# Attention and squared-ReLU feed-forward: fewer DMA transfers per pair of heads

## The chip, the cores and the metric

The kernel runs on one core of a Trainium2 chip. The metric is device time in microseconds (us) of one execution. A core has five engines that run side by side: TensorE (PE in the rows, its weight loads PEld), VectorE (DVE), ScalarE (ACT), GpSimd (POOL) and SyncE (SP), which here only issues DMA transfers. Data lie in DRAM, in the on-chip SBUF, and in the PSUM banks to which TensorE writes.

## The reference

```python
# q, k, v: 8 x 12 heads x 448 x 64; g_q, g_k: 64; w_in: 768 x 2048; w_out: 2048 x 768
def rmsnorm(x, g):
    return x / np.sqrt(np.mean(x * x, axis=-1, keepdims=True) + 1e-06) * g
q_n, k_n = rmsnorm(q, g_q), rmsnorm(k, g_k)
scores = np.matmul(q_n, k_n.transpose(0, 1, 3, 2)) / np.sqrt(64)
scores = scores - np.max(scores, axis=-1, keepdims=True)
attn = np.exp(scores)
attn = attn / (np.sum(attn, axis=-1, keepdims=True) + 1e-09)
attn_out = np.matmul(attn, v)
x = attn_out.transpose(0, 2, 1, 3).reshape(8 * 448, 768)
r = np.maximum(x @ w_in, 0.0)
out = (s * r * r + b) @ w_out
```

## The kernel before

The 96 heads are worked on in 48 pairs p, one head on SBUF partitions 0 to 63 and the other on 64 to 127. After attention come the two products of the feed-forward, `ffn_in` and `multiply`. The change touches attention alone.

Attention runs through slots i, four for each pair (`W = 4`). In a slot TensorE makes one of four blocks of scores (`score`, tile `sh`), VectorE takes the negative row maxima of it (`maximum`, tile `nmx`), TensorE makes a block of transposed scores in full precision and adds the maxima to it by a second matmul (`score_t`, tile `st`, from `kq` and `shq`), ScalarE takes the exponent (`exponent`, tile `e`), and in every odd slot TensorE multiplies two such blocks with `v` and with ones, which gives the sums (`weigh`, tile `av`). All instructions of an engine run in the order in which `slot` writes them. `score` runs up to `AHEAD = 10` slots ahead of `score_t`, because the maxima have to go from 112 partitions to one row of `shq` by two DMA transfers (`shift`, L253). `sh` has one buffer: the next scores wait until VectorE has read the last ones. `nmx` has two buffers, so the first maximum of pair p + 2 waits until both transfers of pair p have read their tile; `shq` has three.

What else a pair needs, in slots counted from its own, is set by `STAGES` and by the lines `at(...)`: the raw rows of k and q are loaded (`load`, L180, tile `raw`, two buffers), squared on ScalarE (L186) and summed on VectorE (L191); GpSimd makes 1/rms (`norm`, L193 and L194, tile `ri`), which goes to DRAM (`keep`, L197, `i_d`) and comes back spread over partitions (`spread`, L210, two transfers, tile `rb`, two buffers); k and q are also loaded transposed (`load_kq`, L204, tile `kq`, six buffers), multiplied by the norms on GpSimd (`scale`, L217) and rounded on ScalarE (L222, tile `kr`); v comes by L226. Afterwards ScalarE copies sums and products out of `av` (`take`, L303 and L304, tiles `sz` and `uz`), four small transfers bring the sums to 128 partitions (`gather`, L312, tile `zt`), VectorE inverts them (`invert`), they go to DRAM (`put_z`, L324) and come back spread (`get_z`, L329, two transfers, `zb`), GpSimd divides (`divide`, L335) and the result goes to DRAM (`put_x`, L338). Every second pair or so a piece of `w_in` is loaded (`convert`, L345) and split.

Every one of these transfers is issued by SyncE, one after the other, in the order of the code. A transfer has one of eight semaphores (DMAHW0 to DMAHW7), given out in turn; the queue that issues waits, where its semaphore is still taken, until the transfer that had it eight places before has landed. It also waits there for the engine that makes the data or frees the buffer, and everything behind it in the queue waits too.

Of the kernel before, what the change touches and what calls it, by code (L numbers as in the profile page):

```python
# [48 lines left out]
def attention_then_relu2_ffn(  # L49
    ctx: ExitStack,  # L50
    tc: tile.TileContext,
    kq: bass.AP,
    kq_rows: bass.AP,
    v: bass.AP,
# [11 lines left out]
    NPAIR, P, _, SEQ = kq.shape  # L66
    NT, DM = out.shape
    DF = w_in.shape[1]
    B = NT // SEQ
    D = P // 2  # L70
    NP = NPAIR // B
    TILES = 2 * SEQ // P
# [27 lines left out]
    x_d = [dpool.tile([NP, P, SEQ], F32, name=f"x_d{b}") for b in range(B)]  # L100
    z_d = [dpool.tile([2, SEQ], F32, name=f"z_d{p}") for p in range(NPAIR)]
# [53 lines left out]
    def attention(ps):  # L155
# [22 lines left out]
        def load(p):  # L178
            raw = raws[p] = ep.tile([P, 2, TILES, D], F32, tag="raw", bufs=2, name=f"raw{p}")
            nc.sync.dma_start(raw, kq_rows[p])  # L180
# [15 lines left out]
        def keep(p):  # L196
            nc.sync.dma_start(  # L197
                i_d[p].rearrange("t (p c) -> p t c", c=TILES),
                invs.pop(p).rearrange("p (t c) -> p t c", c=TILES),
            )  # L200

        def load_kq(p):
            t = kqs[p] = ap.tile([P, 2, SEQ], F32, tag="kq", bufs=6, name=f"kq{p}")
            nc.sync.dma_start(t, kq[p])  # L204

        def spread(p):
            rb = rbs[p] = ep.tile([P, 2, SEQ], F32, tag="rb", bufs=2, name=f"rb{p}")
            for j in range(2):
                r = i_d[p][:, j * SEQ : (j + 1) * SEQ].rearrange("(o t) s -> o t s", o=1)
                nc.sync.dma_start(rb[j * D : (j + 1) * D], r.broadcast_to([D, 2, SEQ]))  # L210

        def scale(p):
            t, rb = kqs[p], rbs.pop(p)
            S.activation(t[:, 1], t[:, 1], AF.Copy, scale=gqk)
            for n in range(2):
                E = V if p + n == 0 else G
                E.tensor_tensor(t[:, n], t[:, n], rb[:, n], ALU.mult)  # L217
# [5 lines left out]

        def load_v(p):
            t = vs[p] = ap.tile([P, NKC, 2, D], F32, tag="v", bufs=3, name=f"v{p}")
            nc.sync.dma_start(t, v[p])  # L226
# [13 lines left out]
        def maximum(i):  # L240
            p, c = divmod(i, W)
            if c == 0:
                nmxs[p] = ap.tile([QC, 2, NQ], F32R, tag="nmx", bufs=2, name=f"nmx{p}")
# [55 lines left out]
        def take(p):  # L299
            t = avs.pop(p)  # L300
            uz = uzs[p] = lp.tile([P, SEQ], F32, tag="uz", bufs=3, name=f"uz{p}")
# [4 lines left out]
        def gather(p):  # L306
            zt = zts[p] = lp.tile([P, 2, TILES], F32, tag="zt", bufs=2, name=f"zt{p}")
            sz = szs.pop(p)
            for j in range(2):
                for h in range(2):  # L310
                    n = (2 * h + j) * Q
                    nc.sync.dma_start(  # L312
# [508 lines left out]
```

## Time and profile before

| | |
|---|---|
| time, median of 3 runs | 1506.2 us (1504.15 to 1506.61) |
| time of the profiled execution | 1501.29 us |
| its span, first to last instruction | 1499.5 us |
| TensorE busy | 1399.3 us, 93% |
| VectorE, ScalarE, GpSimd busy | 759.2, 661.0, 622.0 us |
| mean granted TensorE clock | 0.973 |
| transfers by queue | all program transfers on one queue |

Busy time is the time in which an engine has an instruction under way; issuing transfers and waiting count for none. The attention part ends about 598 us after the first instruction; the feed-forward takes the rest. The time of an execution is 1.8 us longer than the span.

### The profile page before, as it was taken

To read this page: it belongs to the slowest core of one execution; us is meant where nothing else is said; L and a number is where in the kernel's file an instruction comes from. 1 tells how busy PE (TensorE), PEld (TensorE's weight loads), DVE (VectorE), ACT (ScalarE), POOL (GpSimd) and SP (SyncE) were. 2 spreads that over 40 slices of the span, in tenths; PEclk is the share of its full clock that TensorE was granted. 3 is DMA by queue.
4 is the path that set the end of the run, shared out by engine and by line. 5 is a ranking of instruction groups with operands and counts; after the bars stand their busy time and mean duration, and the time that the engine had idled before them with its cause. 6 is when DMAs were issued, how large, how long until landed. Compare 5 with 4: busy or idle time off the path is not lost. (4 is left out here: it accounts for less than half of the span.)

```text
span 1499.5 us, 23471 instructions
## 1 busy us (share of the span) xinstructions
PE 1399.3 (93%) x8536; PEld 1076.7 (72%) x8536; DVE 759.2 (51%) x1113; ACT 661.0 (44%) x1010; POOL 622.0 (41%) x536
## 2 busy tenths in 40 slices
PE   2799998888888999999999999999899999999999
PEld 2343443333333444799999999999799999999999
DVE  3465555555555653121222222224597777767775
ACT  3376566655656555222222222223554444444443
POOL 6466666666666652000000000004666546555653
PEclk6799999999999999999999999999999999999999
DMA  6567777767677774344434434434443324333331
GB/s 188 151 179 199 202 205 204 207 199 199 184 199 200 215 199 124 119 143 145 146 115 152 155 109 152 146 104 155 136 120 106 94 85 120 99 92 104 102 98 63
DMA packets 191235, 221.76 MB, mean 148 GB/s; under 512 B 69520, under 2 KB 162192, under 8 KB 191120
## 3 DMA queue, kind: packets, MB, share of 16 engines
q1 hardware_dynamic: 191120, 220.26, 49.7%
q8 instruction: 67, 1.10, 0.3%
q14 instruction: 48, 0.39, 0.1%
HBM read 161.48 MB, written 58.19 MB: 146 GB/s over the span
## 5 line engine op out<-in xcount | busy, mean ns | idle before, releaser
L439 PE MATMUL ph<-x,wih 128*128 128x448 f32 x1536 | 436.4, 365 | 1.1 <-ACT uz L304 1.1
L619 PE MATMUL m<-t,gh 128*128 128x384 f32 x1568 | 400.5, 336 | 7.3 <-ACT gh L600 7.3
L244 DVE TENSOR_REDUCE nmx<-sh 112x2 fp32r<-112x896 f32 x192 | 208.3, 1086 | 223.3 <-PE sh L235 107.6
L439 PEld LDWEIGHTS ph<-x,wih 128*128 128x128 f32 x1536 | 288.5, 188 | 24.7 <-ACT uz L304 1.9
L619 PEld LDWEIGHTS m<-t,gh 128*128 128x128 f32 x1568 | 284.5, 188 | 7.7 <-ACT gh L600 7.7
L439 PE MATMUL ph<-x,wil 128*128 128x448 f32 x768 | 280.5, 365 | 0.0
L275 ACT ACTIVATE e<-st 128x896 f32<-128x896 f32 x192 | 176.0, 917 | 216.0 <-PE st L268 215.6
L619 PE MATMUL m<-t,gl 128*128 128x384 f32 x784 | 263.3, 336 | 0.3 <-DVE gl L601 0.2
L457 ACT ACTIVATE r<-ph 128x448 f32<-128x448 f32 x128 | 69.6, 545 | 324.9 <-PE ph L439 175.3
L235 PEld LDWEIGHTS sh<-kr 64*112 64x112 f32 x384 | 54.2, 277 | 183.6 <-DVE nmx L244 77.3
L600 ACT CAST gh<-g 128x896 fp32r<-128x896 f32 x112 | 105.5, 943 | 177.9 <-POOL g L590 105.1
L527 POOL TENSOR_TENSOR w<-w 128x384 f32<-128x384 f32 x13 | 16.4, 1263 | 397.8 <-DMA w<-w_d 396.5
L264 PE MATMUL st<-kq 64*128 64x448 f32 x768 | 179.7, 544 | 0.0
L235 PE MATMUL sh<-kr 64*112 64x448 f32 x384 | 98.0, 507 | 83.2 <-DVE nmx L244 36.6
L285 PE MATMUL av<-e,v 128*32 128x448 f32 x1536 | 174.5, 574 | 0.0
L601 DVE TENSOR_TENSOR gl<-g,gh 128x896 fp32r<-128x896 f32 x112 | 141.9, 1268 | 57.2 <-ACT gh L600 52.4
L586 POOL TENSOR_TENSOR g<-g 128x256 f32<-128x256 f32 x112 | 94.5, 844 | 179.6 <-DVE g L585 179.6
L439 PEld LDWEIGHTS ph<-x,wil 128*128 128x128 f32 x768 | 144.2, 188 | 11.4
L619 PEld LDWEIGHTS m<-t,gl 128*128 128x128 f32 x784 | 147.5, 188 | 1.2 <-DVE gl L601 1.2
L268 PE MATMUL st<-shq,row 64*128 64x448 f32 x384 | 139.2, 717 | 3.1 <-DMA shq<-nmx 3.1
L430 DVE TENSOR_TENSOR x<-xr,x 128x448 fp32r<-128x448 f32 x48 | 30.4, 635 | 207.9 <-ACT x L429 207.9
L590 POOL TENSOR_TENSOR g<-g 128x256 f32<-128x256 f32 x112 | 133.9, 1196 | 0.0
(64 smaller groups left out, 1452.1 us busy)
## 6 DMA issues: line engine op xcount, KB each, us to landing
r_d<-r SPq DMA_DIRECT2D x128, 224.0 KB, 2.0
raw<-in_dram SPq DMA_DIRECT2D x48, 448.0 KB, 6.1
kq<-in_dram SPq DMA_DIRECT2D x48, 448.0 KB, 3.8
rb<-i_d SPq DMA_DIRECT2D x96, 224.0 KB, 5.1
raw<-r_d SPq DMA_DIRECT2D x64, 256.0 KB, 2.8
v<-in_dram SPq DMA_DIRECT2D x48, 256.0 KB, 2.9
w64i<-in_dram SPq DMA_DIRECT2D x24, 512.0 KB, 5.1
w64o<-in_dram SPq DMA_DIRECT2D x32, 384.0 KB, 3.3
```

The source lines that it names most:

```text
L235: T.matmul(sh[:QC, j, :SEQ], t[d, 1].rearrange("k (p c) -> k c p", c=NQ)[:, c], t[d, 0], start=True, stop=True,)
L244: V.tensor_reduce(out=nmxs[p][:, :, c : c + 1], in_=shs.pop(i)[:QC, :, :SEQ], op=ALU.max, axis=AX.X, negate=True,)
L264: T.matmul(st[:, j, :SEQ], t[d, 0, k0 : k0 + P], t[d, 1], start=True, stop=False)
L268: T.matmul(st[:, j, :SEQ], row[d], shq[p % 3][d], start=False, stop=True)
L275: S.activation(e, sts.pop(i)[:, :, :SEQ], AF.Exp)
L285: T.matmul(t[n * Q : (n + 1) * Q, 0, :SEQ], x[:, 2 * g + h, j, m * Q : (m + 1) * Q], e[h][:, j], start=g + h == 0, stop=g + h == 2,)
L439: T.matmul(ph[:, :SEQ], w[:, cc, f0 : f0 + P], xs[b, cc][:, part, :], start=cc == 0 and n == 0, stop=cc == NCC - 1 and n == 2,)
L586: G.tensor_tensor(g9[:, 2:4], g9[:, 0:2], g9[:, 7:8].broadcast_to([P, 2, P]), ALU.add)
L590: G.tensor_tensor(g9[:, 5:7], g9[:, 0:9:8], g9[:, 1:8:6], ALU.subtract)
L600: S.copy(gh, g9[:, 1:8])
L601: V.tensor_tensor(gl, g9[:, 1:8], gh.bitcast(F32), ALU.subtract)
L619: T.matmul(to, g[:, sa], w, start=m == 0 and n == 0, stop=m == NM - 1 and n == 2,)
```

## The change

Six edits, all in attention. (1) The four transfers of `gather` become two: the four rows of `sz` go to a new DRAM tile `s_d`, and two slots later a new function `fetch` reads them to 128 partitions; `invert` to `put_x` come two slots later, and `uz` gets a fourth buffer. (2) The transposed k and q and the v of a pair lie side by side in DRAM and come in one load of 5632 bytes for each partition; `load_v` is gone, and v stays in the `kq` tile, which is now used until the last `weigh` of its pair. (3) From pair 4 on the raw rows are loaded by ScalarE's queue instead of SyncE's. (4) The norms go to DRAM in one run of 14 numbers for each partition instead of two of 7, in another order; `spread` reads one run for each partition, and `scale` reads `rb` with a stride. (5) `nmx` gets four buffers instead of two. (6) Slots go on for two more steps of the feed-forward.

```diff
--- before.py
+++ after.py
@@ -98,6 +96,7 @@
 
     r_d = [dpool.tile([NFC, P, SEQ], F32, name=f"r_d{b}") for b in range(B)]
     x_d = [dpool.tile([NP, P, SEQ], F32, name=f"x_d{b}") for b in range(B)]
+    s_d = [dpool.tile([4, SEQ], F32, name=f"s_d{p}") for p in range(NPAIR)]
     z_d = [dpool.tile([2, SEQ], F32, name=f"z_d{p}") for p in range(NPAIR)]
     w_d = [dpool.tile([2, P, 2, DM // 2], F32, name=f"w_d{m}") for m in range(NFC // 2)]
     i_d = [dpool.tile([2, 2 * SEQ], F32, name=f"i_d{p}") for p in range(NPAIR)]
@@ -177,7 +176,7 @@
 
         def load(p):
             raw = raws[p] = ep.tile([P, 2, TILES, D], F32, tag="raw", bufs=2, name=f"raw{p}")
-            nc.sync.dma_start(raw, kq_rows[p])
+            (nc.sync if p < 4 else nc.scalar).dma_start(raw, kq_rows[p])
 
         def norm(p):
 
@@ -195,35 +194,35 @@
 
         def keep(p):
             nc.sync.dma_start(
-                i_d[p].rearrange("t (p c) -> p t c", c=TILES),
-                invs.pop(p).rearrange("p (t c) -> p t c", c=TILES),
+                i_d[p].rearrange("j (p n) -> (j p) n", n=2 * TILES), invs.pop(p)
             )
 
         def load_kq(p):
-            t = kqs[p] = ap.tile([P, 2, SEQ], F32, tag="kq", bufs=6, name=f"kq{p}")
-            nc.sync.dma_start(t, kq[p])
+            t = ap.tile([P, 2 * SEQ + 2 * NKC * D], F32, tag="kq", bufs=6, name=f"kqv{p}")
+            nc.sync.dma_start(t, kqv[p])
+            kqs[p] = t[:, : 2 * SEQ].rearrange("p (n s) -> p n s", n=2)
+            vs[p] = t[:, 2 * SEQ :].rearrange("p (c j d) -> p c j d", j=2, d=D)
 
         def spread(p):
-            rb = rbs[p] = ep.tile([P, 2, SEQ], F32, tag="rb", bufs=2, name=f"rb{p}")
+            rb = rbs[p] = ep.tile([P, 2 * SEQ], F32, tag="rb", bufs=2, name=f"rb{p}")
             for j in range(2):
-                r = i_d[p][:, j * SEQ : (j + 1) * SEQ].rearrange("(o t) s -> o t s", o=1)
-                nc.sync.dma_start(rb[j * D : (j + 1) * D], r.broadcast_to([D, 2, SEQ]))
+                nc.sync.dma_start(
+                    rb[j * D : (j + 1) * D], i_d[p][j : j + 1].broadcast_to([D, 2 * SEQ])
+                )
 
         def scale(p):
-            t, rb = kqs[p], rbs.pop(p)
+            t = kqs[p]
+            rb = rbs.pop(p).rearrange("p (s t c) -> p t s c", t=2, c=TILES)
             S.activation(t[:, 1], t[:, 1], AF.Copy, scale=gqk)
             for n in range(2):
                 E = V if p + n == 0 else G
-                E.tensor_tensor(t[:, n], t[:, n], rb[:, n], ALU.mult)
+                of = t[:, n].rearrange("p (s c) -> p s c", c=TILES)
+                E.tensor_tensor(of, of, rb[:, n], ALU.mult)
             yield
             yield
             yield
             kr = krs[p] = ep.tile([P, 2, SEQ], F32R, tag="kr", bufs=2, name=f"kr{p}")
             S.copy(kr, t)
-
-        def load_v(p):
-            t = vs[p] = ap.tile([P, NKC, 2, D], F32, tag="v", bufs=3, name=f"v{p}")
-            nc.sync.dma_start(t, v[p])
 
         def score(i):
             p, c = divmod(i, W)
@@ -240,7 +239,7 @@
         def maximum(i):
             p, c = divmod(i, W)
             if c == 0:
-                nmxs[p] = ap.tile([QC, 2, NQ], F32R, tag="nmx", bufs=2, name=f"nmx{p}")
+                nmxs[p] = ap.tile([QC, 2, NQ], F32R, tag="nmx", bufs=4, name=f"nmx{p}")
             V.tensor_reduce(
                 out=nmxs[p][:, :, c : c + 1], in_=shs.pop(i)[:QC, :, :SEQ],
                 op=ALU.max, axis=AX.X, negate=True,
@@ -298,21 +297,17 @@
 
         def take(p):
             t = avs.pop(p)
-            uz = uzs[p] = lp.tile([P, SEQ], F32, tag="uz", bufs=3, name=f"uz{p}")
+            uz = uzs[p] = lp.tile([P, SEQ], F32, tag="uz", bufs=4, name=f"uz{p}")
             sz = szs[p] = lp.tile([P, SEQ], F32, tag="sz", bufs=2, name=f"sz{p}")
             S.copy(sz, t[:, 1, :SEQ])
             S.copy(uz, t[:, 0, :SEQ])
 
         def gather(p):
+            nc.sync.dma_start(s_d[p], szs.pop(p)[0:P:Q])
+
+        def fetch(p):
             zt = zts[p] = lp.tile([P, 2, TILES], F32, tag="zt", bufs=2, name=f"zt{p}")
-            sz = szs.pop(p)
-            for j in range(2):
-                for h in range(2):
-                    n = (2 * h + j) * Q
-                    nc.sync.dma_start(
-                        zt[j * D : (j + 1) * D, h],
-                        sz[n : n + 1].rearrange("o (p c) -> o p c", c=TILES),
-                    )
+            nc.sync.dma_start(zt, s_d[p].rearrange("(h j) (p c) -> (j p) h c", h=2, c=TILES))
 
         def invert(p):
             zt = zts[p]
@@ -366,13 +361,13 @@
             ):
                 at(max(slot_of(s0) + off, FIRST + least + p), f, p)
             at(slot_of(s0 + W - 1) + (p > 0), shift, p)
-            at(max(s0 - 4, FIRST + 10), load_v, p)
             at(s0 + 7, gather, p)
-            at(s0 + 10, invert, p)
-            at(s0 + 11, put_z, p)
-            at(s0 + 13, get_z, p)
-            at(s0 + 16, divide, p)
-            at(s0 + 18, put_x, p)
+            at(s0 + 9, fetch, p)
+            at(s0 + 12, invert, p)
+            at(s0 + 13, put_z, p)
+            at(s0 + 15, get_z, p)
+            at(s0 + 18, divide, p)
+            at(s0 + 20, put_x, p)
         for n in range(len(pieces)):
             at(8 + 7 * n, convert, n)
 
@@ -700,7 +695,7 @@
             rectify()
             ffn_in(b, fc)
             keep_r()
-            if n < 20:
+            if n < 22:
                 slot(NSLOT + 2 + n)
             else:
                 begun[:] = [g for g in begun if next(g, 0) is None]
@@ -803,7 +798,8 @@
 
     vs[:, : p // 2, 3] = 0
     g = _np.stack([_np.tile(_np.asarray(inputs[x]), 2) for x in ("g_q", "g_k")], 1)
-    laid = [kq, rows, vs, g] + [_np.asarray(inputs[x]) for x in _INS]
+    kqv = _np.concatenate([a.reshape(n, p, -1) for a in (kq, vs)], 2)
+    laid = [kqv, rows, g] + [_np.asarray(inputs[x]) for x in _INS]
     arrays, args = {}, []
     for i, a in enumerate(laid):
         a = _np.ascontiguousarray(a)
```

SyncE's queue, before, from the spread norms of pair 14 to the sums of pair 8 (names end in a buffer number of the build; `x2` is a repetition; in brackets the semaphores that the queue waits for ahead of the transfer: DMAHW is an earlier transfer, the others are engines):

```order
L210 DMA rb_1439<-i_d_161 64x2x448 [waits DMAHW6_49,Pool_49]
L210 DMA rb_1439<-i_d_161 64x2x448 [waits DMAHW7_49]
L180 DMA raw_1442<-in_dram 128x896 [waits DMAHW0_49,DVE_49]
L338 DMA x_d_83<-u_1413 128x448 [waits DMAHW1_49,Pool_49]
L253 DMA shq_217<-nmx_1345 1x112x4 [waits DMAHW2_49,DVE_49]
L253 DMA shq_217<-nmx_1345 1x112x4 [waits DMAHW3_49,PE_49]
L197 DMA i_d_162<-ri_1377 128x2x7 [waits DMAHW4_49]
L324 DMA z_d_98<-zt_1381 128x7 [waits DMAHW5_49,DVE_49]
L312 DMA zt_1498<-sz_1457 64x1x7 [waits DMAHW6_49,Activation_49]
L312 DMA zt_1498<-sz_1457 64x1x7 [waits DMAHW7_49]
L312 DMA zt_1498<-sz_1457 64x1x7 [waits DMAHW0_49]
L312 DMA zt_1498<-sz_1457 64x1x7 [waits DMAHW1_49]
```

The same place now, from the load of pair 14 on:

```order
L202 DMA kqv_1422<-in_dram 128x1408 [waits DMAHW6_49,PE_49]
L340 DMA w64i_1424<-in_dram 128x1024 [waits DMAHW7_49]
L319 DMA z_d_145<-zt_1325 128x7 [waits DMAHW0_49,DVE_49]
L310 DMA zt_1439<-s_d_98 128x2x7 [waits DMAHW3_49,DMAHW1_49]
L209 DMA rb_1444<-i_d_209 64x896 [waits DMAHW2_49]
L209 DMA rb_1444<-i_d_209 64x896
L252 DMA shq_265<-nmx_1354 1x112x4 [waits DMAHW4_49,DVE_49]
L252 DMA shq_265<-nmx_1354 1x112x4 [waits DMAHW5_49]
L196 DMA i_d_210<-ri_1385 128x14 [waits DMAHW6_49,Pool_49]
L324 DMA zb_1501<-z_d_145 64x448 [waits DMAHW7_49,DMAHW0_49]
L324 DMA zb_1501<-z_d_145 64x448
L306 DMA s_d_99<-sz_1462 4x448 [waits DMAHW1_49,Activation_49]
```

The loads of `v` and `raw` and two of the four `zt` transfers are gone from the queue, `s_d` is new, and the one load `kqv` waits for TensorE: for the last matmul with v of the pair six before, which stands one slot later in the program than the load.

ScalarE's instructions, before, from the scaling of the `kq` of pair 14, in the odd slot in which the sums and products of pair 9 are copied out of `av`:

```order
L214 ACTIVATE kq_1417<-kq_1417,gqk 128x448 [waits DMAHW2_49]
L303 COPY sz_1571<-av_1503 128x448 [waits DMAHW6_49,DMAHW5_49,DMAHW7_49,DMAHW0_49,PE_49]
L304 COPY uz_1570<-av_1503 128x448 [waits Pool_49]
L275 ACTIVATE e_1584<-st_1579 128x896 [waits PE_49,Activation_49]
L110 ACTIVATE wih_223<-w64i_1419 128x512 [waits DMAHW3_49]
L186 ACTIVATE raw_1442<-raw_1442 128x896 [waits DMAHW0_49]
L275 ACTIVATE e_1601<-st_1596 128x896 [waits PE_49,Activation_49]
```

And now:

```order
L216 ACTIVATE kqv_1422<-kqv_1422,gqk 128x448 [waits DMAHW6_49]
L179 DMA raw_1557<-in_dram 128x896 [waits DMAHW3_49,DVE_49]
L302 COPY sz_1572<-av_1505 128x448 [waits PE_49]
L303 COPY uz_1571<-av_1505 128x448 [waits Pool_49]
L274 ACTIVATE e_1585<-st_1580 128x896 [waits PE_49]
L109 ACTIVATE wih_271<-w64i_1424 128x512 [waits DMAHW7_49]
L185 ACTIVATE raw_1447<-raw_1447 128x896 [waits DMAHW5_49]
```

The load of `raw` (pair 18) stands between the scaling of `kqv` and the two copies out of `av`; it waits for VectorE, which has to have summed the buffer's last rows, and for DMAHW3, which the transfer eight places before has, counted over both queues: here the second `rb` of pair 14. Of the 44 such loads 22 stand behind an `rb`, 11 behind an `shq`, 6 behind a `w64i`.

## Rows read from the trace of the kernel before

**Rows 1.** Windows: busy us (instructions) by engine, clock, DMA share, GB/s; stages.

```profile
0.00:85.00 85.00, 45.09 (x284) 25.67 (x284) 36.34 (x43) 32.19 (x41) 42.63 (x43) 0.76 0.59 166
85.00:125.00 40.00, 40.00 (x322) 18.35 (x320) 27.58 (x36) 28.71 (x40) 29.65 (x20) 1.00 0.72 199
125.00:545.00 420.00, 372.19 (x2772) 163.07 (x2770) 237.52 (x323) 250.39 (x353) 264.64 (x195) 0.96 0.72 200
500.00:550.00 50.00, 45.81 (x350) 20.31 (x342) 28.97 (x39) 29.02 (x42) 30.06 (x23) 0.97 0.79 212
545.00:598.00 53.00, 52.65 (x424) 22.84 (x420) 23.64 (x36) 30.63 (x42) 15.78 (x13) 1.00 0.52 154
598.00:1499.50 901.50, 889.38 (x4750) 846.73 (x4748) 434.16 (x678) 319.10 (x535) 269.29 (x268) 1.00 0.38 119
```

**Rows 2.** Waits from 125 to 545: us in total, times, longest.

```profile
DVE nmx L244 <- DMA shq<-nmx: 98.2, 24, 6.1
...
PEld sh L235 <- DVE nmx L244: 65.2, 32, 4.1
```

**Rows 3.** Timeline of TensorE's `av` matmuls, ahead of a wait and behind it.

```profile
307.81 1.71 PE L285 MATMUL av<-e,v 128*32 128x448 f32 x16
...
316.21 2.95 PE L285 MATMUL av<-e,v 128*32 128x448 f32 x16
```

**Rows 4.** Timeline of SyncE's queue, one pair: start, us, transfers.

```profile
449.80 0.53 SPq L226 DMA_DIRECT2D v<-in_dram  x1
450.42 0.38 SPq L204 DMA_DIRECT2D kq<-in_dram  x1
450.89 1.10 SPq L329 DMA_DIRECT2D zb<-z_d  x2
452.08 1.27 SPq L210 DMA_DIRECT2D rb<-i_d  x2
453.44 1.44 SPq L180 DMA_DIRECT2D raw<-in_dram  x1
454.97 0.38 SPq L338 DMA_DIRECT2D x_d<-u  x1
455.45 1.24 SPq L253 DMA_DIRECT2D shq<-nmx  x2
456.74 0.58 SPq L197 DMA_DIRECT2D i_d<-ri  x1
457.38 0.46 SPq L345 DMA_DIRECT2D w64i<-in_dram  x1
457.93 0.38 SPq L324 DMA_DIRECT2D z_d<-zt  x1
458.40 3.13 SPq L312 DMA_DIRECT2D zt<-sz  x4
461.63 0.53 SPq L226 DMA_DIRECT2D v<-in_dram  x1
```

**Rows 5.** Transfers from 125 to 545: count, KB each, median us from issue to landing.

```profile
rb<-i_d SPq DMA_DIRECT2D x69, 224.0 KB, 5.2
...
zt<-sz SPq DMA_DIRECT2D x140, 1.8 KB, 2.9
shq<-nmx SPq DMA_DIRECT2D x70, 1.8 KB, 5.8
```

**Rows 6.** Groups of instructions on GpSimd, 600 to 1499: busy us, mean ns.

```profile
L590 POOL TENSOR_TENSOR g<-g 128x256 f32<-128x256 f32 x112 | 133.9, 1196 | 0.0
```

**Rows 7.** The same view from 125 to 545.

```profile
L217 POOL TENSOR_TENSOR kq<-kq,rb 128x448 f32<-128x448 f32 x70 | 83.3, 1209 | 9.9 <-PE st L268 3.3 <-ACT kq L214 2.8 <-DMA rb<-i_d 2.4
```

**Rows 8.** Timeline of the start: first scores, first shift, first use of it.

```profile
22.25 0.94 ACT L222 CAST kr<-kq 128x896 fp32r<-128x896 f32 x1 [0.16 <-POOL kq L217]
...
38.17 1.23 SPq L253 DMA_DIRECT2D shq<-nmx  x2
...
44.10 1.01 PE L268 MATMUL st<-shq,row 64*128 64x448 f32 x2 [3.11 <-DMA shq<-nmx]
```

More of the change, by code (lines that the diff above doesn't have):

```diff
@@ L51, in attention_then_relu2_ffn @@
     tc: tile.TileContext,
-    kq: bass.AP,
+    kqv: bass.AP,
     kq_rows: bass.AP,
-    v: bass.AP,
     g_qk: bass.AP,
@@ L64, in attention_then_relu2_ffn @@
     V, S, G, T = nc.vector, nc.scalar, nc.gpsimd, nc.tensor
-    NPAIR, P, _, SEQ = kq.shape
     NT, DM = out.shape
     DF = w_in.shape[1]
+    NPAIR, P, _, TILES, D = kq_rows.shape
+    SEQ = TILES * P // 2
     B = NT // SEQ
-    D = P // 2
     NP = NPAIR // B
-    TILES = 2 * SEQ // P
     NQ = 4
```

## The prediction

> **What bounds the kernel now.** I read the windows by stage first [rows 1]. The feed-forward, from 598 us on, has TensorE busy 889.4 of 901.5 us at full clock, and the change does not touch it. The start, 0 to 85, is a chain of loads and norms. Between lie two kinds of attention. From 85 to 125 TensorE is busy all of 40.0 us and gets through 322 matmuls; a pair has 80 (8 `sh`, 16 and 8 `st`, 32 and 16 `av`), so a pair takes 10.0 us. From 545 to 598, 424 matmuls in 53 us: again 10.0 us for a pair. Between them, from 125 to 545, 2772 matmuls take 420 us. That is 34.65 pairs of 12.12 us. All three stretches hold the same work for TensorE, and the first has the pieces of `w_in` in it too, so 10.0 us is what TensorE needs and 34.65 x 2.12 = 73.5 us are lost in the middle.
>
> The same row says how: 420 - 372.2 = 47.8 us TensorE is idle, and the other 25.7 us are work that took longer. The granted clock is 0.96 there and 1.00 in the stretches beside it, and behind an idle time the 16 `av` matmuls take 2.95 us in place of 1.71 [rows 3]: the lower of the two levels, 1.2 in place of 2.4 GHz, for a while after each longer wait. So a wait costs about half as much again as it lasts, and both parts go if it goes.
>
> What TensorE waits for is VectorE's maximum (65.2 us of waits ahead of `sh`), and VectorE in turn waits 24 times, 98.2 us, up to 6.1 us each, for the transfers of `shift` [rows 2]: the first maximum of a pair finds both `nmx` buffers taken, because the shift of the pair two before has not read its tile. That shift was due four slots earlier. It is late because SyncE's queue is full [rows 4]: from one `v` load to the next are 11.83 us, and transfers stand end to end in them, 10.89 us with gaps of some 0.1 us between. Two places in it are waits rather than issue: `raw` has 1.44 us where `v`, a load of the same kind, has 0.53, and the four `zt` 3.13 us. A shift also needs 5.8 us from issue to landing though it carries 1.8 KB [rows 5]; it stands behind the large loads.
>
> **The change part by part.** Off SyncE's queue, per pair, by the durations of [rows 4]: the `v` load, 0.53; the `raw` load, 1.44 with its wait (0.53, as `v`, without); two of four `zt`, 1.57 (3.13 / 2). `s_d` and the new `zt` count as the two that stay. With four gaps of 0.1 that is 3.0 to 3.9 us less of 11.83, so 7.9 to 8.8 us for a period that needs 10.0. The merged `kqv` load is priced between 0.38 and 0.53 (the `kq` and `v` rows); the store of norms at most its 0.58, the rows of half the count. I take 8.5 us: SyncE falls below TensorE, and the slack is 1.5 us a pair.
>
> `nmx` with four buffers removes the wait itself: the first maximum of a pair now needs the shift of the pair four before, eight slots (some 20 us) more. What is late next is TensorE's second `st` matmul, which needs the shifted row in `shq`, six slots or 15 us after the shift's place. With 5.8 us to land that allows SyncE to run 9 us late. So with the queue at 8.5 us of 10.0 I put both stalls at nothing.
>
> New waits. The `kqv` load has to wait until TensorE has done the last `av` of the pair six before, one slot after its own place, so SyncE runs at least a slot (2.5 us) behind once a pair. Behind it stand `z_d`, `zt`, both `rb`, both `shq`, `i_d`. They have the 9 us above (`shq`), and `rb` is issued about 3 us after the release and lands at 8.2 (5.2 in [rows 5]), ahead of the multiplication four slots after it, at 10. Cost nothing, up to 0.6 us a pair if the larger load in front delays them. The sums now go by two transfers in sequence. The first is bounded by the small ones of [rows 5], 2.9 and 5.8 us, and the second follows two slots (5 us) behind: at most 0.8 us of wait, inside SyncE's slack; the second has three slots (7.5 us). Nothing.
>
> ScalarE issues `raw` itself: 0.38 to 0.53 us, as `kq` and `v` on SyncE [rows 4], on an engine that is busy 250.4 / 34.65 = 7.2 us a pair [rows 1]; hidden in the 2.8 us that are left of 10.0. But it also waits there, ahead of the two copies out of `av`, for a transfer of SyncE's. ScalarE comes there some 10 us after the `kqv` release of the pair before; the second `rb`, 22 loads of 44, has landed at 8.2, so no wait; an `shq`, 11 loads, is issued near 4.3 and lands at 10.1: a wait of a few tenths to 1 us. Averaged with the delays above I put 0.15 us a pair on it, bounds 0 and 0.6.
>
> GpSimd multiplies with a strided `rb`. Nothing here shows that form. Contiguous it takes 1209 ns for 448 elements [rows 7]; the dearest strided one, in the feed-forward, 1196 ns for 256 [rows 6], which would be 2.09 us for 448. GpSimd is busy 264.6 / 34.65 = 7.6 us a pair; twice 0.88 more is 9.4, still below 10.0. I take the lower, since the runs of seven stay contiguous; the upper one goes into the range.
>
> The start: the first `kr` ends at 23.2, the first shift is issued at 38.2 and lands at 44.1, when TensorE can go on [rows 8]. The early `kqv` loads carry 256 KB more each, at the 166 GB/s of that stretch 1.5 us, and ScalarE's two extra waits stand ahead of its first `kr`. Against it SyncE has two `raw` loads less ahead of the first shift. I take +2 us, bounds -5 and +6.
>
> Sum, against the profiled execution: 34.65 pairs x (12.12 - 10.15) = 68.3 us less, 2 more at the start: 1501.3 - 68.3 + 2 = 1435.0 us. The median of the three runs, 1506.2, lies 4.9 above the profiled one; stalls of varying length would do that, and most are to go, so I add 2: **1437 us**.
>
> **A rule against it.** The DMA share is 0.72 from 125 to 545 [rows 1], which leaves room, while SyncE's queue has none [rows 4]; the sum above goes by that. The Trainium skill, "DMA: Bandwidth & Descriptors", section "Issuing engines are not separate DMA queues", says that transfers of all issuing engines share the same 16 DMA engines, and that another issuer saves only the sequencer's time, "usually small relative to the DMA itself". Here that time is the larger part, as rows 4 show; were it small, the move of `raw` would bring nothing and the merged load its half microsecond alone. No run here yet shows which holds once the queue is relieved; it is the first rival.
>
> **The rivals.** (a) The transfers themselves become the bound. The DMA engines are busy 0.72 x 420 / 34.65 = 8.7 us a pair; at 10.0 that would be 0.87, and the fullest 50 us show 0.79 [rows 1]. If 0.79 is as far as it goes, a pair takes 8.7 / 0.79 = 11.05 us: 34.65 x 1.07 = 37 us less, and with the start 1466. Against it: the merged loads and the norms' longer runs need fewer packets for the same bytes. This is the rule's case. Chance 0.25, 1448 to 1482.
>
> (b) The change does not do what it says: SyncE's waits grow by what the issues shrink, because the eight semaphores allow only eight transfers under way, and the period stays at 11.8 or so; TensorE then waits for `shq` in place of `sh`. For it: the waits in `zt` and `raw`. Against: 13.6 transfers a pair take the place of 16.6. 34.65 x 0.1 to 0.5: 1485 to 1503. Chance 0.06.
>
> (c) Slower: ScalarE stands at the `raw` load. Its period is 7.2 + 0.5 + the wait. It is as long as now when the wait is 4.4 us, that is when an `rb` needs 10 - 3 + 4.4 = 11.4 us to land where 5.2 are seen. At 12.5 us the pair takes 13.2, 34.65 x 1.1 = 38 us more: 1540. For it: `kqv` and `raw` are issued at nearly the same time, 1152 KB together, and all small transfers stand behind. Against: a landing time twice what any row shows. Chance 0.07.
>
> **How the numbers follow.** The forecast, a pair of 10.0 to 10.4 us, has 0.60; with its bounds (73.5 less and 5 at the start; 0.4 x 34.65 = 14 and 6 more) it runs from 1423 to 1448. The remaining 0.02 is for less than that. To leave out no more than two in ten the range takes in (a): 1424 to 1480. Faster by over 0.2% (3 us, about what a measurement of this kernel can tell from no change): 0.60 + 0.25 + 0.05 of (b), and 0.01 of the rest, 0.91. Within 0.2%: 0.02. Slower: 0.07.
>
> **What would show it.** Right: the 2772 matmuls of the middle in about 350 us, clock near 1.00, no wait of VectorE for `shq<-nmx`, gaps in SyncE's queue ahead of each `kqv`, ScalarE's wait at the `raw` load below 1 us. (a) shows a DMA share near 0.8 with landing times well above those of rows 5; (b) SyncE without gaps and TensorE waiting at `st` for `shq`; (c) ScalarE idle at that load and TensorE idle at `av` or `st` behind it. Two things would make the forecast wrong without any of these: a start much longer than 85 us, and GpSimd's strided product near 2 us with the waits around it.

## The result, and the profile after

The changed kernel takes 1446.5 us (median of 4 runs, 1442.0 to 1450.5) where the kernel before takes 1505.2 on the same chip (1499.7 to 1506.6): a ratio of 0.9616, with an interval of 0.9572 to 0.9659. The forecast was 1437, in a range of 1424 to 1480. The profiled execution took 1443.12 us; the forecast's sum for it was 1435.0. In one kernel of the table below, e10_raw_later, two of six executions fell into a slower state of the chip (1555.6 and 3523.5 us) and are left out of its numbers.

The windows by stage come first, as for before in [rows 1]; the middle is cut at 500 here, because the last 45 us of it run free of stalls now.

```profile
core 0: us, PE busy (x) PEld busy (x) DVE busy (x) ACT busy (x) POOL busy (x), PEclk, DMA share, GB/s
0.00:85.00 85.00, 44.83 (x278) 25.43 (x280) 35.75 (x40) 31.97 (x41) 41.37 (x43) 0.76 0.61 177
85.00:125.00 40.00, 40.00 (x322) 18.48 (x322) 26.99 (x36) 28.56 (x40) 29.80 (x22) 1.00 0.75 219
125.00:500.00 375.00, 359.56 (x2864) 168.35 (x2868) 247.32 (x333) 258.36 (x363) 298.45 (x197) 1.00 0.80 229
500.00:545.00 45.00, 45.00 (x370) 19.13 (x362) 18.06 (x28) 25.10 (x35) 11.65 (x10) 1.00 0.39 112
```

Between 125 and 500 there are 2864 matmuls, 35.8 pairs of 10.47 us, where a pair took 12.12. The 34.65 pairs that the forecast counted take 57.2 us less by that, and the profiled execution is 58.2 us shorter: nearly the whole gain lies in the middle. The start is much what it was (278 matmuls in the first 85 us, 284 before). The granted clock of the middle is 1.00 again (0.96 before), and TensorE's busy time is 359.56 / 35.8 = 10.04 us a pair, the 10.0 that the forecast said it needs. What is left of the loss is idle time alone: 375 - 359.56 = 15.4 us.

The waits from 125 to 545 say who holds it (us in total, times, longest; to be read against [rows 2]):

```profile
DVE nmx L243 <- PE sh L234: 87.6, 119, 1.8
...
DVE zt L314 <- DMA zt<-s_d: 37.2, 22, 3.9
POOL u L330 <- DMA zb<-z_d: 34.6, 17, 8.7
...
POOL kqv L220 <- DMA rb<-i_d: 26.2, 18, 3.9
...
PE sh L234 <- DVE nmx L243: 12.9, 13, 2.0
...
DVE zt L314 <- DMA rb<-i_d: 9.1, 7, 2.9
```

VectorE's 98.2 us of waits for `shq` are gone; its maxima wait for TensorE's scores, as they should. It waits instead at `invert` (line 314) for the sums that now come by way of DRAM, 22 times, up to 3.9 us. The 9.1 us that the view puts down to `rb` are waits for the sums too: the instruction reads `zt` alone. I went through TensorE's idle times of over 0.3 us from 85 to 545: there are 14, 14.4 us together, and 13 of them follow a wait of VectorE at line 314, behind the late maximum. The other one waits for ScalarE's copy `uz`.

The views give no landing times for the changed kernel, but the semaphores' updates in the trace do. Counted with 5 updates for an `s_d` and 16 for every other transfer, the updates of all eight semaphores come out even, and in 28 of the 29 waits at line 314 VectorE starts 0.02 to 0.1 us behind the landing of `zt` found in this way. Landing times of the changed kernel and the runs below are counted so, as means from issue to landing for issues between 125 and 500.

SyncE's queue in such a pair, start and us, to be read against [rows 4]:

```profile
335.71 0.54 SPq L306 DMA_DIRECT2D s_d<-sz  x1
336.55 0.32 SPq L333 DMA_DIRECT2D x_d<-u  x1
336.97 0.38 SPq L202 DMA_DIRECT2D kqv<-in_dram  x1
337.44 0.40 SPq L319 DMA_DIRECT2D z_d<-zt  x1
339.98 0.37 SPq L310 DMA_DIRECT2D zt<-s_d  x1
340.40 1.46 SPq L209 DMA_DIRECT2D rb<-i_d  x2
341.91 1.23 SPq L252 DMA_DIRECT2D shq<-nmx  x2
344.65 0.33 SPq L196 DMA_DIRECT2D i_d<-ri  x1
346.26 1.12 SPq L324 DMA_DIRECT2D zb<-z_d  x2
347.47 0.54 SPq L306 DMA_DIRECT2D s_d<-sz  x1
```

Issue no longer fills the queue: the rows add up to 6.2 us of the 11.8 from one `s_d` to the next, with gaps of 2.1 us ahead of `zt<-s_d`, 1.5 ahead of `i_d` and 1.3 ahead of `zb`. Over the whole middle, 125 to 500, the issues add up to 6.69 us a pair (8.98 before). The rest is not room, for SyncE stands in most of it: its waits for earlier transfers to land went from 1.9 us a pair to 2.8 (59 and 102 us in all). In the first of those gaps SyncE waits for a piece of `w64i` and last for `s_d`, which releases the fetch 4.3 us after its own issue. The timeline of the other engines, same pair, with the idle time and its releaser in brackets (the first row, a pair earlier, is the copy whose sums the `s_d` at 335.71 stores):

```profile
327.04 0.54 ACT L302 COPY sz<-av 128x448 f32<-128x448 f32 x1
...
346.40 0.17 DVE L314 SCALAR_TENSOR_TENSOR zt<-zt 128x7 f32<-128x7 f32 x1 [2.53 <-DMA zt<-s_d]
...
346.72 1.04 DVE L243 TENSOR_REDUCE nmx<-sh 112x2 fp32r<-112x896 f32 x1
...
347.26 0.34 ACTq L179 DMA_DIRECT2D raw<-in_dram  x1
...
347.69 0.53 ACT L302 COPY sz<-av 128x448 f32<-128x448 f32 x1 [0.51 <-DMA shq<-nmx]
...
347.90 0.56 PE L234 MATMUL sh<-kr 64*112 64x448 f32 x2 [1.00 <-DVE nmx L243]
```

The fetch issued at 339.98 lets VectorE go at 346.40, 6.4 us later. VectorE had stood there for 2.53 us, the maximum behind it is late, and TensorE's next score waits 1.00 us. In the bracket at 347.69 ScalarE's half microsecond at the `raw` load is seen as well. And SyncE comes late to `s_d` itself: the copy that it stores ended at 327.58, and it is issued at 335.71, 8.1 us later, where its place in the program is two slots, 5.2 us, behind. From 125 to 500 these are 8.7 us on average.

### The profile page after: what moved, and what is told of

It is laid out like the page before. It is cut to its first block, busy times and chain, and to the rows that moved or that the text cites. A ratio compares the mean times of both kernels' runs of the same rounds, so it can differ in the third digit from the quotient of the medians.

```text
span 1441.3 us, 22975 instructions
## 1 busy us (share of the span) xinstructions
PE 1375.1 (95%) x8536; PEld 1077.4 (75%) x8536; DVE 764.3 (53%) x1113; ACT 660.9 (46%) x1010; POOL 651.4 (45%) x536
## 4 chain that ended last, share of the span: by engine, by line
PE 79%; DMA 11%; DVE 3%; POOL 2%; ACT 2%; issue 1%; SPq 1%; ACTq 0%; POOLq 0%; DVEq 0%
PE ph L434 29%; PE m L614 28%; PE av L284 7%; PE st L263 7%; PE sh L234 3%; PE av L291 3%; DMA zt<-s_d 3%; PE st L267 2%; DMA s_d<-sz 2%; DVE nmx L243 1%; DMA z_d<-zt 1%; DMA kqv<-in_dram 1%; DMA w<-w_d 1%; DMA shq<-nmx 1%; DMA i_d<-ri 1%
## 5 line engine op out<-in xcount | busy, mean ns | idle before, releaser
L263 PE MATMUL st<-kqv 64*128 64x448 f32 x768 | 180.5, 544 | 0.0
L581 POOL TENSOR_TENSOR g<-g 128x256 f32<-128x256 f32 x112 | 94.4, 843 | 179.7 <-DVE g L580 179.7
L284 PE MATMUL av<-e,kqv 128*32 128x448 f32 x1536 | 164.2, 545 | 1.6 <-ACT uz L303 1.6
L434 PEld LDWEIGHTS ph<-x,wil 128*128 128x128 f32 x768 | 144.3, 188 | 11.4
L193 POOL TENSOR_TENSOR ri<-ri,mhalf 128x14 f32<-128x14 f32 x48 | 147.5, 3073 | 4.0
L220 POOL TENSOR_TENSOR kqv<-kqv,rb 128x448 f32<-128x448 f32 x95 | 123.7, 1321 | 39.0 <-DMA rb<-i_d 26.5
```

What stands on the lines that cost most here:

```text
L193: G.tensor_tensor(ri, ri, mhalf[:, :n], ALU.pow)
L220: E.tensor_tensor(of, of, rb[:, n], ALU.mult)
L263: T.matmul(st[:, j, :SEQ], t[d, 0, k0 : k0 + P], t[d, 1], start=True, stop=False)
L284: T.matmul(t[n * Q : (n + 1) * Q, 0, :SEQ], x[:, 2 * g + h, j, m * Q : (m + 1) * Q], e[h][:, j], start=g + h == 0, stop=g + h == 2,)
L434: T.matmul(ph[:, :SEQ], w[:, cc, f0 : f0 + P], xs[b, cc][:, part, :], start=cc == 0 and n == 0, stop=cc == NCC - 1 and n == 2,)
```

## The experiments

The table has every run, ordered by ratio. Ratios are against the kernel before on the same chip (1505.1 to 1509.2 us by job), with their intervals. Matmuls are those from 125 to 500 in the windows; us a pair is 375 / (matmuls / 80); transfers are SyncE's issues in that stretch, counted in the timeline, for a pair.

| kernel | us | ratio | interval | matmuls | us a pair | DMA share | transfers |
|---|---|---|---|---|---|---|---|
| before | 1505.2 | 1 | | 2466 | 12.17 | 0.72 | 16.7 |
| e1_nmx_alone | 1508.0 | 1.0016 | 1.0001 to 1.0031 | 2434 | 12.33 | 0.70 | 16.6 |
| e3_gather_direct | 1479.6 | 0.9829 | 0.9804 to 0.9853 | 2590 | 11.58 | 0.73 | 14.6 |
| e6_heavy | 1476.9 | 0.9810 | 0.9791 to 0.9829 | 2648 | 11.33 | 0.83 | 12.5 |
| e8_norms_two | 1458.6 | 0.9692 | 0.9659 to 0.9724 | 2748 | 10.92 | 0.82 | 12.6 |
| e4_invert_later | 1451.0 | 0.9628 | 0.9604 to 0.9653 | 2804 | 10.70 | 0.82 | 12.4 |
| e2_nmx_two | 1449.6 | 0.9625 | 0.9597 to 0.9653 | 2792 | 10.74 | 0.81 | 12.6 |
| e5_spaced | 1448.2 | 0.9622 | 0.9603 to 0.9641 | 2848 | 10.53 | 0.79 | 12.6 |
| after | 1446.5 | 0.9616 | 0.9572 to 0.9659 | 2864 | 10.47 | 0.80 | 12.6 |
| e10_raw_later | 1445.3 | 0.9588 | 0.9569 to 0.9607 | 2830 | 10.60 | 0.84 | 12.6 |
| e9_split_loads | 1442.7 | 0.9569 | 0.9547 to 0.9591 | 2894 | 10.37 | 0.82 | 13.6 |
| e11_sync_spaced | 1442.6 | 0.9562 | 0.9545 to 0.9579 | 2878 | 10.42 | 0.82 | 13.6 |
| e12_gather_alone | 1441.5 | 0.9549 | 0.9530 to 0.9569 | 2888 | 10.39 | 0.87 | 14.5 |
| e7_raw_sync | 1434.6 | 0.9528 | 0.9508 to 0.9548 | 2950 | 10.17 | 0.88 | 13.4 |

**The buffers of maxima.** My theory was that SyncE's full queue is the cause and the two `nmx` buffers only the place where it shows; the rival, that the buffers are the cause. Two runs: the kernel before with four buffers, and the changed kernel with two.

```diff
-                nmxs[p] = ap.tile([QC, 2, NQ], F32R, tag="nmx", bufs=2, name=f"nmx{p}")
+                nmxs[p] = ap.tile([QC, 2, NQ], F32R, tag="nmx", bufs=4, name=f"nmx{p}")
```

> The kernel before with four buffers of maxima and nothing else. Theory (SyncE's queue is full at 11.4 to 11.8 us a pair, the two buffers only show it): VectorE's waits for shq<-nmx go, TensorE waits at the second st matmul for shq in their place, the middle stretch stays at 11.4 to 12.0 us a pair, and the time is 1485 to 1503 us. Rival (the two buffers were the loss): the middle at 10.0 to 10.6 us a pair and 1430 to 1455 us.

> The changed kernel with two buffers of maxima as before; all transfers as changed. Theory (a relieved queue makes the shift nearly in time): some waits of VectorE for shq<-nmx come back, 0 to 1 us in most pairs, and the time is 5 to 20 us above the changed kernel, 1450 to 1467 us. Rival (the buffers were the loss): 1485 us or more.

Four buffers alone gain nothing (1.0016), and two in the changed kernel cost 3.1 us, inside the intervals. Two of VectorE's waits in the kernel before, 125 to 500, and then the waits of the first run:

```profile
DVE nmx L244 <- DMA shq<-nmx: 89.6, 22, 6.1
...
DVE zt L319 <- DMA zt<-sz: 6.5, 11, 1.5
```

```profile
DVE zt L319 <- DMA zt<-sz: 89.2, 30, 5.5
...
PEld sh L235 <- DVE nmx L244: 70.9, 40, 4.3
...
DVE nmx L244 <- DMA shq<-nmx: 1.8, 1, 1.8
```

The wait for `shq` went from 89.6 us in that stretch to 1.8, and nearly as many microseconds came back at `invert` (6.5 to 89.2). I had expected it at `st`; the next thing that VectorE needs from SyncE's queue came first. The theory of the full queue stands, and the rival falls.

**The sums by way of DRAM, undone.** The four direct transfers again, at their old places in the schedule, with the other edits kept.

```diff
         def gather(p):
-            nc.sync.dma_start(s_d[p], szs.pop(p)[0:P:Q])
-
-        def fetch(p):
             zt = zts[p] = lp.tile([P, 2, TILES], F32, tag="zt", bufs=2, name=f"zt{p}")
-            nc.sync.dma_start(zt, s_d[p].rearrange("(h j) (p c) -> (j p) h c", h=2, c=TILES))
+            sz = szs.pop(p)
+            for j in range(2):
+                for h in range(2):
+                    n = (2 * h + j) * Q
+                    nc.sync.dma_start(
...
-            at(s0 + 12, invert, p)
+            at(s0 + 10, invert, p)
```

> The changed kernel with the sums gathered by four direct transfers at the old places (invert to put_x two slots earlier); the other edits stay. Theory (what TensorE still loses is VectorE's wait for the sums that come by way of DRAM, zt<-s_d, 37 us, and SyncE has room): VectorE's waits for zt fall below 15 us, the two further transfers fill some of SyncE's slack, and the time is within 6 us of the changed kernel, 1436 to 1452 us. Rival (fewer transfers is what counts, each place in the queue is worth its time): the middle at 11 us a pair or more and 1462 us or above.

It takes 1479.6 us, 33 more than the changed kernel, and my theory fell: this edit had looked like two places in a queue with room to spare.

```profile
DVE zt L318 <- DMA zt<-sz: 71.7, 25, 4.7
...
PEld sh L234 <- DVE nmx L243: 58.2, 53, 3.3
ACT sz L302 <- DMA zt<-sz: 44.3, 23, 3.7
...
PE sh L234 <- DVE nmx L243: 27.0, 22, 2.5
...
PE av L284 <- ACT uz L303: 11.4, 15, 1.8
```

VectorE stands at `invert` for 71.7 us (in the changed kernel 44.6 in the same stretch: 35.5, and 9.1 put down to `rb`), and ScalarE now stands ahead of its copy `sz` as well, 44.3 us, behind transfers of SyncE's (its `raw` load is the instruction before). TensorE pays for both, more for VectorE's late maxima (27.0) than for ScalarE's late `uz` (11.4).

**The sums by way of DRAM, alone.** The reverse: the kernel before with this edit only, and the later steps and the fourth `uz` buffer that go with it.

```diff
         def gather(p):
-            zt = zts[p] = lp.tile([P, 2, TILES], F32, tag="zt", bufs=2, name=f"zt{p}")
-            sz = szs.pop(p)
...
+            nc.sync.dma_start(s_d[p], szs.pop(p)[0:P:Q])
...
+            at(s0 + 9, fetch, p)
-            at(s0 + 10, invert, p)
+            at(s0 + 12, invert, p)
...
```

> The kernel before with the sums gathered by way of DRAM, their later steps and the fourth uz buffer as changed, nothing else: two places less in SyncE's queue for each pair. Theory (places bound the kernel before): 11.0 to 11.4 us a pair in the middle, 1465 to 1482 us. Rival (the direct gather hurts only together with the merged load): 1495 to 1508 us.

1441.5 us: this edit alone brings all of the gain, 23 us more than I had expected at best. The waits of its middle:

```profile
DVE nmx L245 <- DMA shq<-nmx: 31.5, 13, 4.5
...
DVE zt L316 <- DMA zt<-s_d: 7.6, 7, 2.9
...
DVE nmx L245 <- PE st L269: 4.0, 2, 2.1
```

With two `nmx` buffers the wait for `shq` is still there, a third of what it was, and the pair takes 10.39 us. The prediction's own queue arithmetic says this much: 1.57 us for two `zt` and 0.2 for their gaps, off 12.12 to 12.17, is 10.35 to 10.40. I had not used it when I wrote the expectation, since I took the sums for a small part of the whole. The trace bears it out as a total: SyncE's issues go from 8.98 to 7.39 us a pair. The transfers themselves are 1.1 of these 1.6 (four of 0.52 on average against 0.54 and 0.45); why the rest became shorter is not shown. The sums by way of DRAM cost VectorE 7.6 us of waits here, where they cost 44.6 in the changed kernel.

**`raw` on SyncE's queue.** The changed kernel with the raw rows issued by SyncE throughout.

```diff
-            (nc.sync if p < 4 else nc.scalar).dma_start(raw, kq_rows[p])
+            nc.sync.dma_start(raw, kq_rows[p])
```

> The changed kernel with the raw rows back in SyncE's queue, the other edits kept. Theory (each place in SyncE's full queue is worth 0.55 to 0.85 us a pair, by the two places of the direct gather): 11.0 to 11.3 us a pair and 1462 to 1476 us. Rival (another issuing engine saves next to nothing): 1441 to 1452 us.

This is the kernel with the lowest time, 1434.6 us, 12 less than the changed kernel, although SyncE issues about one transfer a pair more. Its window and SyncE's waits, 125 to 500, and then SyncE's waits of the changed kernel in the same stretch:

```profile
125.00:500.00 375.00, 369.30 (x2950) 171.91 (x2942) 251.74 (x341) 263.48 (x372) 291.64 (x203) 1.00 0.88 235
...
DVE zt L314 <- DMA zt<-s_d: 22.9, 16, 3.6
...
SPq L310 <- DMA s_d<-sz: 6.8, 9, 1.6
```

```profile
SPq L310 <- DMA s_d<-sz: 37.4, 20, 2.7
SPq L324 <- DMA z_d<-zt: 26.5, 21, 2.6
```

With `raw` on ScalarE's queue SyncE waits 37.4 us for `s_d` to land, with `raw` on its own 6.8. VectorE's wait at `invert` falls from 44.6 us in that stretch to 32.0 (9.1 of either put down to `rb`), and among ScalarE's waits those for SyncE's transfers ahead of `sz` are no longer listed. The DMA share is higher, 0.88, and the kernel is faster: 0.80 was no ceiling. The transfers issued beside the `raw` load on ScalarE's queue land later there: `s_d` 3.4 us after its issue against 2.8 here, `kqv` 6.8 against 5.7, `z_d` 6.7 against 5.8. Others land earlier: `shq` 5.1 against 6.1.

**The bytes on ScalarE's queue.** Is it the bytes of `raw` beside SyncE's, or the wait on ScalarE? 256 KB more in each `raw` load.

```diff
+            m = n if p < 4 else n + MORE
-            (nc.sync if p < 4 else nc.scalar).dma_start(raw, kq_rows[p])
+            (nc.sync if p < 4 else nc.scalar).dma_start(raw[:, :m], kq_rows[p][:, :m])
```

> The changed kernel with 256 KB more in each load of raw rows on ScalarE's queue from pair 4 on (the further columns are not used); places in the queues are the same. Theory (places and landing waits of SyncE's queue are the limit, bandwidth is not): 10.5 to 10.9 us a pair, 1444 to 1462 us, the DMA share up to 0.85 to 0.88. Rival (the DMA engines are full at 0.80 to 0.82): the share stays and a pair takes 11.2 to 11.6 us, 1470 to 1485 us.

```profile
DVE zt L318 <- DMA zt<-s_d: 73.4, 29, 4.7
...
PE sh L238 <- DVE nmx L247: 29.8, 22, 2.8
...
PE av L288 <- ACT uz L307: 7.7, 7, 2.0
...
SPq L314 <- DMA s_d<-sz: 44.9, 20, 3.6
```

1476.9, 30 us more. The DMA share rises only from 0.80 to 0.83, and VectorE's wait for the sums grows to 73.4 us. My theory, that bytes have room, fell; the rival's time and pair come out, though not its ground, a share that cannot rise (e7_raw_sync has 0.88). The run does not part the two by its edit, since ScalarE's idle time ahead of `sz` grows too, from 23.8 us to 49.7. TensorE's waits part them: 29.8 us are for VectorE's late maxima (12.9 in the changed kernel), 7.7 for ScalarE's `uz` (1.6). So the greater part of these bytes' price goes by the sums, and the transfers do land later: `s_d` 3.9 us after its issue (3.4 in the changed kernel), the fetch 5.9 (5.3), `z_d` 7.6 (6.7).

**The norms in two runs**, on their old layout, with the contiguous product on GpSimd:

```diff
-                i_d[p].rearrange("j (p n) -> (j p) n", n=2 * TILES), invs.pop(p)
+                i_d[p].rearrange("t (p c) -> p t c", c=TILES),
+                invs.pop(p).rearrange("p (t c) -> p t c", c=TILES),
```

> The changed kernel with the norms stored in two runs and spread as before, and scale without a stride; places in the queue as changed. Theory (places count, packets hardly): i_d and rb issues longer by 0.05 to 0.1 us each, 10.5 to 10.8 us a pair, 1445 to 1460 us; GpSimd's product without stride at 1.13 to 1.25 us where it is 1.3. Rival (the DMA engines are full and packets count): 11 us a pair and 1462 us or more.

1458.6, 12 us more, with an interval that meets that of the changed kernel at 0.9659: as far as that shows, the longer runs are worth their cost on GpSimd there. That is not so everywhere: e12_gather_alone also has the norms in two runs, with `raw` on SyncE's queue, and is as fast as any but one.

**`k`, `q` and `v` in two loads** from the one array:

```diff
-            nc.sync.dma_start(t, kqv[p])
+            nc.sync.dma_start(t[:, : 2 * SEQ], kqv[p][:, : 2 * SEQ])
+            nc.sync.dma_start(t[:, 2 * SEQ :], kqv[p][:, 2 * SEQ :])
```

> The changed kernel with the one load of k, q, v cut in two, k and q first, v behind it, same tile and same bytes: one place more in SyncE's queue for each pair. Theory (a place is worth 0.4 to 0.6 us a pair, half of what the two places of the direct gather cost): 10.9 to 11.1 us a pair and 1460 to 1470 us. Rival (bytes and their order are what counts, not places): 1441 to 1452 us.

1442.7 and 0.9569, not slower at all; my theory fell. SyncE's issues grow by 0.6 us a pair, from 6.69 to 7.28, and its waits for landings shrink by 0.8, from 2.8 to 2.0: one place more costs nothing where its issue fills a wait.

**Later steps.** Can VectorE's remaining wait be had by giving the sums more time? First `invert` and what follows it two slots later, with a fifth `uz` buffer; then fetch five slots behind gather and the same for the rows behind `put_z`; then that with `raw` on SyncE's queue. The cut shows the first. The other two put `fetch` at `s0 + 12` and `invert` at `s0 + 14`, so they give `s_d` more time to land and the fetch less, two slots where it had three.

```diff
-            at(s0 + 12, invert, p)
+            at(s0 + 14, invert, p)
...
```

> The changed kernel with invert and all that follows it two slots later, and a fifth uz buffer; the same transfers. Theory (13 of the 14 idle times of TensorE above 0.3 us follow VectorE's wait for zt<-s_d ahead of invert): these waits fall below 8 us in total, TensorE's middle stretch goes from 10.5 to 10.0 to 10.1 us a pair, and the time is 12 to 18 us below the changed kernel, 1426 to 1436 us. Rival (the waits are a sign of a queue that is still late, so the next thing in order waits): no change beyond 5 us, 1441 to 1451 us.

> The changed kernel with the two trips through DRAM stretched: fetch five slots behind gather instead of two, get_z five behind put_z instead of two, divide and put_x after them, five uz buffers; the same transfers and bytes. Theory (SyncE is still the limit, and 2 to 2.5 us of its 10.5 us a pair it stands at the head of the queue for the landing of s_d and z_d, because too few places lie between store and load): these two waits fall below 0.5 us a pair, TensorE gets its 10.0 to 10.15 us a pair, and the time is 1426 to 1437 us. Rival (the DMA engines at a share of 0.80 to 0.82 are full): the share stays there, the waits move to other places, 10.4 to 10.7 us a pair and 1441 to 1452 us.

> The raw rows back in SyncE's queue and the trips through DRAM stretched, both at once: the candidate for the best version. Theory (what is left of TensorE's idle time follows VectorE's wait for the sums): 10.0 to 10.1 us a pair, 1426 to 1433 us. Rival (stretching moves waits, as it did with the raw rows on ScalarE's queue): 1432 to 1438 us, no gain over the raw rows in SyncE's queue alone.

None gains: 0.9628, 0.9622 and 0.9562. In the first the wait at `invert` is gone, 1.1 us of it are left, and these stand in its place:

```profile
PEld av L284 <- ACT uz L303: 28.7, 25, 2.6
...
ACT sz L302 <- DMA x_d<-u: 23.2, 12, 2.9
PE av L284 <- ACT uz L303: 21.6, 21, 2.3
```

TensorE waits for ScalarE's copy out of `av`, and ScalarE for SyncE's transfers at its `raw` load. In the second the wait at `invert` is little shorter than it was (37.6 us, 21 times): the fetch has a slot less, and SyncE, relieved of the waits for `s_d`, stands at others (32.4 us ahead of `x_d` for GpSimd's product, 20.8 ahead of `kqv` for TensorE). So more time for the sums cures VectorE's wait where it is given, in the first, but not the time of the kernel while `raw` is on ScalarE's queue. The first with `raw` on SyncE's queue was not run.

**`raw` on ScalarE's queue, two slots later**, away from `kqv`:

```diff
-    "raw": (-21, 0),
+    "raw": (-19, 0),
```

> The changed kernel with the load of raw rows still on ScalarE's queue, but two slots later (offset -19 in place of -21), so that it is issued some 4 us behind kqv and s_d instead of beside them, and in a slot without copies out of av. Theory (the raw rows from ScalarE's queue go out just as SyncE stores s_d and loads kqv, and delay the landing of s_d at which SyncE stands): SyncE's waits for s_d fall below 0.6 us a pair, 10.1 to 10.3 us a pair, 1430 to 1440 us, as with the raw rows in SyncE's queue. Rival (two queues at once are the worse way whenever they run): 1441 to 1452 us.

0.9588, between the changed kernel and the one with `raw` on SyncE, whose interval it does not reach.

```profile
SPq L196 <- DMA kqv<-in_dram: 34.9, 22, 3.6
...
SPq L310 <- DMA s_d<-sz: 5.1, 10, 1.4
```

SyncE's wait for `s_d` is down to 5.1 us, as expected, `s_d` lands 2.6 us after its issue, and ScalarE waits ahead of `sz` for TensorE alone (5.3 us). Yet a pair takes 10.60 us, and VectorE waits 39.1 us at `invert` (3.4 of them put down to `rb`): SyncE now stands ahead of `i_d` until `kqv` lands. So with the wait for `s_d` and ScalarE's both gone, most of the loss is still there; by what the second queue costs it stays open.

## Why the prediction was nearly right, and where it was not

The time came out within 10 us in part by luck. TensorE's 10.0 us a pair leave no more than 2.1 of 12.12 to be had, so that the sum came near as soon as one term was enough; the others could be wrong in it without moving it far, and most were.

**What bounds the kernel** held. TensorE needs 10.0 us a pair (busy 10.04 after), the clock came back to 1.00 with the waits gone, and the middle was late because of SyncE's deliveries and not for want of buffers (e1_nmx_alone and e2_nmx_two). That the wait itself goes with four buffers held too: `shq` is missing among VectorE's waits. How the queue was full was read from one pair, in which 10.89 of 11.83 us count as transfers; rows with x2 and x4 there hold the waits between their transfers. Over the whole middle the issues alone are 8.98 us of 12.17, and the waits for landings 1.9.

**The two `zt` transfers** were priced at 1.57 us a pair, and by e12_gather_alone a pair takes 1.78 less with that edit alone, 12.17 to 10.39, its two gaps included. As a total this term was right, and it is all that was needed; how it is made up was not foreseen (1.1 us of their own issue, the rest elsewhere in the queue).

**The `raw` load, "1.44 with its wait", failed.** The prediction counted it as time off SyncE's queue. It came off the queue, and the kernel is 12 us slower for it (e7_raw_sync). The 1.44 was moreover the longest issue of its kind in the kernel before, 125 to 545 (shortest, median and longest in ns):

```profile
L180 SPq DMA_DIRECT2D raw<-in_dram x34: 334/543/1436, 125.3 to 523.9; - x34
```

The rule that the prediction set against itself, the Trainium skill, "DMA: Bandwidth & Descriptors", section "Issuing engines are not separate DMA queues", has all issuers' transfers interleave on the same DMA engines, the issuer saving only sequencer time. The runs agree in that `raw` on another issuer brought nothing; that it cost 12 us is more than the rule says. That the engines' share itself is the bound, which was rival (a), does not hold: 0.88 goes with the fastest kernel and 0.80 with the changed one, and `shq` lands no later than in [rows 5] (median 5.0 us, 5.8 there). What the bytes beside SyncE's do is shown by e6_heavy, 30 us for 256 KB; by what the move of `raw` alone costs 12 us is not shown, since e10_raw_later has neither SyncE's wait for `s_d` nor ScalarE's ahead of `sz` and is hardly faster.

**The merged load**, 0.53 us, brought nothing (e9_split_loads), and **the norms in one run**, taken at no gain to speak of, are worth some 12 us while `raw` is on ScalarE's queue (e8_norms_two, where the intervals meet). Together the edits beside the first one have no gain: 0.9549 without them, 0.9616 with them, 0.9528 with all but the move of `raw`; the first and the last overlap. After the first edit, 0.4 us a pair was all that was left above TensorE's 10.0.

**"Nothing" for the sums in two transfers failed**, and it is the size that the forecast is off by. The trip itself fitted: from the issue of `s_d` to the landing of the fetch are 9.1 us on average (10.7 in the pair shown), within five slots of 13 us. What failed is the slack of 1.5 us, by which SyncE was to be in time. It issues `s_d` 8.7 us behind the end of ScalarE's copy instead of 5.2; its 6.69 us of issue a pair come with 3.8 of other time, 2.8 of it waits for landings. VectorE's 46.3 us of waits at `invert`, 125 to 545, and, through them, 13 of TensorE's 14 idle times are this term. In e12_gather_alone, with the same two transfers at the same places, SyncE issues `s_d` 7.2 us behind the copy, the sums land 8.4 us after that, and VectorE's waits there are 7.6 us. A pair of 10.47 us in place of 10.15, times 34.65, is 11.1 us; the start, put at +2, hardly grew; 1435.0 + 11.1 - 2 is 1444.1, and the profile has 1443.1. The offset of the median, +2, measured 3.4.

**ScalarE's wait** was put at 0.15 us a pair. ScalarE's idle time ahead of `sz` is 23.8 us from 125 to 500, 5.2 of it for TensorE, and so 0.5 us a pair, close to the upper bound of 0.6; in the changed kernel all but one idle time of TensorE lies elsewhere. Rival (c) did not come near here; its wait at the `raw` load is seen in e3_gather_direct (44.3 us) and e6_heavy. **GpSimd's strided product** takes 1383 ns in the middle where the contiguous took 1218, near the lower bound taken, and GpSimd is busy 298.45 / 35.8 = 8.3 us a pair, below 10.

**Rival (b)**, that SyncE's waits grow by what the issues shrink, is out as a forecast, since a pair takes 10.47 us and not 11.8. In part its mechanism is there: the issues shrank by 2.3 us a pair, and the waits for landings grew by 0.9.

What stays open. The edit that pays has two halves, fewer direct gathers and two slots more before `invert`. e3_gather_direct undid both, and neither half was tried by itself; in the changed kernel two more slots bring nothing (e4_invert_later), and in the kernel before VectorE's waits at `invert`, which they could shorten, are 6.5 us. e3_gather_direct and e12_gather_alone also have nearly the same number of transfers, 14.6 and 14.5 a pair, and stand 38 us apart, so the count does not explain it; that e3 has `raw` on ScalarE's queue and e12 on SyncE's is one difference, the gathers are the other. And the 12 us of the `raw` load: the transfers issued beside it land 0.6 to 1.0 us later, but the run that moves it away from them keeps most of the loss.

## What to carry to other kernels

Where an in-order queue of transfers is full, price each place in it with its waits, from many pairs and not from one, and expect the gain to end where another engine sets the pace: here the first two places paid 1.78 us of 2.1 a pair and the others nothing. Read a gap in such a queue as a wait until the profile says otherwise. Before a large load is moved to another engine's queue, run it both ways: here it cost 12 us. Of several edits made together, run the one that looks smallest alone.

## What was unexpected of the hardware

- A 448 KB load a pair, moved from SyncE's queue to ScalarE's, made the kernel 12 us slower (ratio 0.9528 to 0.9616), and 256 KB more on that queue 30 us slower, at a DMA share of 0.80 to 0.83, while a kernel with all of it on SyncE's queue ran at 0.88.
- A transfer of 7 KB to DRAM landed 3.4 us after its issue on average and 5.0 at most, and the read of the same 7 KB took 5.3 on average and 8.6 at most, with the large loads under way (changed kernel, 125 to 500).
- GpSimd's product on runs of seven, strided, took 1383 ns against 1218 contiguous, 14% more, and an operation of 14 elements beside it, unchanged in the code (the power in `norm`), went from 2713 to 3174 ns; why is not shown.
